# Casts and splits of q and k held behind the maximum and normalising of earlier steps

## The chip, the cores and the metric

The kernel runs on one core of one Trainium2 chip. The metric is the device time of one execution in microseconds; several runs are summed up by their median. The engines are named as in the profile: PE is TensorE, DVE is VectorE, ACT is ScalarE, POOL is GpSimd, and SP is SyncE, which here only issues transfers.

## What is computed

Windowed attention with a distance bias feeds a feed-forward layer with a convolution over the sequence. Sizes are 4 batches, 8 heads, 768 positions, head width 64, 8 global and 96 local keys, model width 512, inner width 1024; all in fp32.

```python
scores = scale * np.matmul(q, k.transpose(0, 1, 3, 2)) + bias     # bias: minus slope x distance
scores = np.where(is_global | is_local, scores, -1e9)
a = np.exp(scores - scores.max(-1, keepdims=True))
x = np.matmul(a / (a.sum(-1, keepdims=True) + 1e-9), v)           # heads side by side: (B, S, 512)
h = np.maximum(x @ w_in, 0.0)
conv_out = sum(conv_w[k] * hp[:, k:k + S] for k in range(3))       # hp: h padded by one row
out = (h / (1.0 + np.exp(-conv_out))) @ w_out
```

## The kernel before

**Tiling.** The attention is 32 jobs m: a batch, a half of its sequence (384 queries) and a pair of heads. A job has three steps of 128 queries, so there are 96 steps s. A step computes scores on TensorE (L372 ff.; L395 from job 9 on), the maximum of each head on VectorE (`maxima`, L404, operation at L412), exponentials on ScalarE (L426), the normalising by the reciprocal (L438) on POOL (L444), and up to step 31 half of it on ScalarE (L442). Two steps later its probabilities are transposed (L452) and evacuated (L457); when the three steps of a job are through, the product with v follows (L473, one PSUM buffer), of which a high part xh (ScalarE, L485) and a low part xl (VectorE, L489) are kept. The scores have two PSUM buffers, so a step's scores wait for the exponentials of the step two before.

**High and low parts.** A product in fp32 is made of three matmuls over rounded high parts and low rests. For the scores of jobs 9 to 31 (NATIVE is 9) `prep(m, part)` (L126) makes them: part 0 casts the keys into kk and the queries into qh on POOL (L137, L138), part 1 subtracts on VectorE, so that the lower half of kk holds the rest (L141), and makes ql (L142). `load(m)` (L93) fetches the raw keys rk and queries rq into one buffer each (L114, L115), `load_v(m)` (L118) fetches v into one of two (L123).

**Feed-forward.** When the four jobs of a half are done, its blocks go through the first product (L507, tile h), the rectifier (ScalarE, L517), three convolution taps (ScalarE L555 or POOL L557, then VectorE L558 and L559), tanh (L577), a check of range (L588), the gate (VectorE, L610), the split into gh (ScalarE, L612) and gl (VectorE, L613), the second product (L622) and its output (L629, L630). The weights are decoded in the first third of the run on VectorE (L316, L318, L320, L331) and POOL (L325); they are read again and compared near the end (L339 to L350).

**Order.** The program's main loop runs over the steps and calls the parts above. Steps below HAND (16) are issued in the order in which they are written. From step 16 on a scheduler orders each engine's queue from the dependences and its own timeline. `tc.issue_after(x)` adds one constraint: what is issued inside it and runs on the engine of x stands behind x in that engine's queue. `last_ttr[s]` is the last maximum of step s, on VectorE.

The loop calls `prep(m + 1)` in the first step of job m, and loads of job m + 2 in its second step (from m = 7 on):

```python
        if i == 0:
            prep(m + 1, 0)
            prep(m + 1, 1)
            if 1 <= m < NATIVE - 2:
                load(m + 2)
        elif i == 1 and m + 2 >= NATIVE:
            load(m + 2)
        if s >= NB and i == 0:
            load_v(m)
```

Of the kernel before, what the change touches and what calls it, by code (L numbers as in the profile page):

```python
# [15 lines left out]
ALU = mybir.AluOpType  # L16
# [9 lines left out]
NB = TB // P  # L26
# [12 lines left out]
HAND = 16  # L39
# [28 lines left out]
def fast_path(tc, io):  # L68
    nc = tc.nc
    V, A, G, T = nc.vector, nc.scalar, nc.gpsimd, nc.tensor  # L70
# [17 lines left out]
    p2 = pool("p2", 2)  # L88

    jobs = [(b, u, hp) for b in range(B) for u in range(2) for hp in range(NPAIR)]  # L90
    raw, qk, vt = {}, {}, {}

    def load(m):  # L93
        if m >= len(jobs):
# [23 lines left out]
    def load_v(m):  # L118
        if m >= len(jobs):
            return  # L120
        b, u, hp = jobs[m]
        t = p2.tile([P, NB, 2, P], F32, tag="v", name=f"v{m}")
        nc.sync.dma_start(t, io["vv"][b, u, hp].rearrange("p (i c d) -> p i c d", i=NB, c=2))  # L123
        vt[m] = t

    def prep(m, part):  # L126
        if m >= len(jobs) or m < NATIVE:
            return
        b, u, hp = jobs[m]
        w = NKC[u]  # L130
        rq, rk = raw[m]
        if part == 0:
            qh = p2.tile([P, 2 * TB], F32R, tag="qh", name=f"qh{m}")
            ql = p2.tile([P, 2 * TB], F32R, tag="ql", name=f"ql{m}")
            kk = p2.tile([P, 2 * w], F32R, tag="kk", name=f"kk{m}")
            qk[m] = (qh, ql, kk)
            G.tensor_copy(kk, rk)  # L137
            G.tensor_copy(qh, rq)  # L138
        else:
            qh, ql, kk = qk[m]  # L140
            V.tensor_tensor(kk[64:], rk[64:], kk[64:].bitcast(F32), ALU.subtract)  # L141
            V.tensor_tensor(ql, rq, qh.bitcast(F32), ALU.subtract)  # L142
# [226 lines left out]
    last_ttr = {}  # L369
# [64 lines left out]
    def normalise(s):  # L434
        pb, c0, n, mm = st_s[s]
        if s >= SHARED:
            V.tensor_scalar(mm[:, 4:6], mm[:, 2:4], 1.0e-9, None, ALU.add)
        V.reciprocal(mm[:, 6:8], mm[:, 4:6])  # L438
        for j in range(2):
            x, inv = pb[:, j, c0 : c0 + n], mm[:, 6 + j : 7 + j]  # L440
            if j and s < SHARED:
                A.activation(x, x, AF.Copy, scale=inv)  # L442
            else:
                G.tensor_scalar(x, x, inv, 1.0, ALU.mult, ALU.mult)  # L444

    def transposes(s):
        m, i = steps[s]
# [43 lines left out]
    def ends(s):  # L491
        return s >= 0 and s % NB == NB - 1
# [218 lines left out]
    def check_some(cost):  # L711
        pace[0] += cost
        while pace[1] < NCHK and pace[0] >= CHECK_EVERY * (pace[1] + 1):
            check_piece(pace[1])
            pace[1] += 1
    last_exp, last_mm, last_ev = {}, {}, {}

    def fill(k):
        with contextlib.ExitStack() as es:
# [65 lines left out]
    for s in range(len(steps) + LAG_V + 1):  # L785
        cur["s"] = s
        m, i = steps[s] if s < len(steps) else (len(jobs), -1)
        if s < HAND:
# [5 lines left out]
            x = (s - LAG_V - 1) // NB if ends(s - LAG_V - 1) else None  # L794
# [8 lines left out]
            if s:  # L803
                normalise(s - 1)
# [17 lines left out]
        else:  # L822
# [20 lines left out]
            if s <= len(steps):  # L843
                normalise(s - 1)
# [18 lines left out]
        if s == 0:  # L863
            for k in range(len(order)):
                chain(*order[k])
        elif s == 1:
            load_v(0)
            load(2)
# [1 line left out]
            if at == s:  # L870
                start_piece(k)
        if i == 0:
            prep(m + 1, 0)
            prep(m + 1, 1)
            if 1 <= m < NATIVE - 2:
                load(m + 2)
        elif i == 1 and m + 2 >= NATIVE:
            load(m + 2)
        if s >= NB and i == 0:
            load_v(m)  # L880
    fill(10**9)
# [133 lines left out]
def build(nc, io):  # L1015
    with tile.TileContext(nc, schedule_with_timeline_sim=True) as tc:
        fast_path(tc, io)
# [49 lines left out]
```

## Time and profile before

| what | value |
|---|---|
| median of 3 runs | 445.34 us (444.66 to 445.89) |
| the profiled execution, its own time | 445.31 us |
| its span, first to last instruction | 443.5 us |
| mean granted TensorE clock | 0.996 of full |
| TensorE busy | 431.2 us (97%) |
| VectorE busy | 357.2 us (81%) |
| ScalarE busy | 309.9 us (70%) |
| POOL busy | 221.2 us (50%) |

Busy times are of one engine; a transfer or another engine may run beside them. Times in the views count from the span's start. Matmuls are pipelined, so the durations of neighbours overlap and the distance of their starts is the shorter, more telling number. A bracket behind an instruction says how long its engine idled before it and which instruction ended that.

### The profile page before, as it was taken

What the parts mean: (1) busy time and instruction counts of PE and PEld (TensorE: products, weight loads), DVE (VectorE), ACT (ScalarE), POOL (GpSimd) and SP (SyncE); (2) the same over time, 40 slices, a digit from 0 to 9 for tenths busy, and PEclk for the clock granted to TensorE, in tenths of its full rate; (3) what the DMA queues carried; (4) which work ended last, traced back from release to release, by engine and by line L of the source; (5) the groups of instructions that cost most, each with busy time, mean ns of one, the idle gap of its engine ahead of it and who ended that gap; (6) DMA issues with size and microseconds to landing.
All of it is one profiled execution on the core that took longest, in us unless ns stands there. A gap on an engine that the chain in (4) does not pass through costs nothing.

```text
span 443.5 us, 9050 instructions
## 1 busy us (share of the span) xinstructions
PE 431.2 (97%) x3039; PEld 374.5 (84%) x3039; DVE 357.2 (81%) x935; ACT 309.9 (70%) x839; POOL 221.2 (50%) x307
## 2 busy tenths in 40 slices
PE   8988999799999999999999999999999999999996
PEld 7655778799889988899889988899988998798876
DVE  6899899998999988757998989747999975568700
ACT  4889988789896678546876865665776776755540
POOL 5555334654456786556757744647656841013000
PEclk9999999899999999999999999999999999999999
DMA  6998953141543244442246134423235313980111
GB/s 210 294 255 258 271 184 110 40 163 65 153 128 120 75 136 132 128 125 94 85 128 192 41 107 145 141 102 104 67 119 181 103 48 122 312 295 32 47 49 55
DMA packets 22662, 60.02 MB, mean 135 GB/s; under 512 B 3024, under 2 KB 5584, under 8 KB 22608
## 3 DMA queue, kind: packets, MB, share of 16 engines
q1 hardware_dynamic: 18992, 53.01, 39.2%
q10 hardware_dynamic: 3616, 6.36, 3.9%
q8 instruction: 26, 0.43, 0.4%
q14 instruction: 28, 0.23, 0.2%
HBM read 53.07 MB, written 6.29 MB: 134 GB/s over the span
## 4 chain that ended last, share of the span: by engine, by line
PE 81%; DVE 8%; DMA 6%; ACT 3%; issue 1%; POOL 0%; SPq 0%; DVEq 0%; ACTq 0%
PE o L622 26%; PE h L507 25%; PE pv L473 10%; PE t L452 9%; PE s L395 7%; DMA check<-in_w 3%; PE s L385 1%; PE last L643 1%; DMA out<-ob 1%; DVE w L320 1%; DVE w L318 1%; ACT junkb L350 1%; ACT pbuf L426 1%; DMA rq<-in_qk 1%; PE sb L385 1%
## 5 line engine op out<-in xcount | busy, mean ns | idle before, releaser
L444 POOL TENSOR_SCALAR pbuf<-pbuf,mm 128x232 f32<-128x232 f32 (+1 forms) x160 | 113.3, 718 | 81.0 <-DVE mm L438 49.5
L426 ACT ACTIVATE pbuf<-s,mm 128x232 f32<-128x232 f32 (+1 forms) x165 | 72.1, 442 | 48.3 <-DVE mm L412 34.6
L412 DVE CUSTOM_DVE_ANT_0 s<-s,tab 128x232 f32<-128x232 f32 (+1 forms) x165 | 63.1, 385 | 20.2 <-PE s L395 15.7
L622 PE MATMUL o<-woh,gh 128*128 128x512 f32 x184 | 74.1, 403 | 0.0
L622 PE MATMUL o<-woh,gl 128*128 128x512 f32 x184 | 73.5, 400 | 0.0
L622 PE MATMUL o<-wol,gh 128*128 128x512 f32 x184 | 73.3, 398 | 0.0
L452 PE MATMUL t<-ident,pbuf 128*128 128x128 f32 x384 | 65.4, 279 | 5.4 <-ACT pbuf L442 2.7
L557 POOL TENSOR_SCALAR c<-hbuf,cw 128x382 f32<-128x382 f32 (+1 forms) x48 | 38.6, 807 | 56.5 <-ACT hbuf L517 56.5
L452 PEld LDWEIGHTS t<-ident,pbuf 128*128 128x128 f32 x384 | 46.4, 141 | 20.2 <-ACT pbuf L442 6.4
L457 ACT ACTIVATE pt<-t 128x512 f32<-128x512 f32 x96 | 57.0, 597 | 8.3 <-PE t L452 8.0
L507 PE MATMUL h<-xl,wih 128*128 128x384 f32 x252 | 59.4, 343 | 0.0
L507 PE MATMUL h<-xh,wih 128*128 128x384 f32 x252 | 58.8, 347 | 0.1
L507 PE MATMUL h<-xh,wil 128*128 128x384 f32 x252 | 55.8, 339 | 0.0
L473 PE MATMUL pv<-pt,v 128*64 128x128 f32 (+1 forms) x768 | 50.3, 280 | 0.3 <-DVE xl L489 0.2
L473 PEld LDWEIGHTS pv<-pt,v 128*64 128x64 f32 (+1 forms) x768 | 42.5, 138 | 8.6 <-issue 3.6
L558 DVE SCALAR_TENSOR_TENSOR c<-hbuf,cw,c 128x382 f32<-128x382 f32 (+1 forms) x64 | 44.3, 699 | 4.8 <-POOL c L557 3.7
L559 DVE SCALAR_TENSOR_TENSOR c<-hbuf,cw,c 128x382 f32<-128x382 f32 (+1 forms) x64 | 45.4, 712 | 0.3
L507 PEld LDWEIGHTS h<-xh,wih 128*128 128x128 f32 x252 | 43.2, 190 | 2.1 <-ACT pbuf L426 0.9
L507 PEld LDWEIGHTS h<-xl,wih 128*128 128x128 f32 x252 | 43.9, 189 | 0.7 <-issue 0.7
L507 PEld LDWEIGHTS h<-xh,wil 128*128 128x128 f32 x252 | 44.1, 188 | 0.0
L517 ACT ACTIVATE hbuf<-h 128x384 f32<-128x384 f32 x64 | 31.4, 495 | 13.5 <-PE h L507 12.5
L622 PEld LDWEIGHTS o<-woh,gl 128*128 128x128 f32 x184 | 34.6, 188 | 7.3
(120 smaller groups left out, 856.1 us busy)
## 6 DMA issues: line engine op xcount, KB each, us to landing
v<-in_vv SPq DMA_DIRECT2D x32, 384.0 KB, 3.6
rq<-in_qk SPq DMA_DIRECT2D x23, 384.0 KB, 3.1
wr<-in_w SPq DMA_DIRECT2D x16, 512.0 KB, 5.3
check<-in_w SPq DMA_DIRECT2D x16, 512.0 KB, 4.9
rk<-in_qk SPq DMA_DIRECT2D x12, 504.0 KB, 3.6
out<-ob ACTq DMA_DIRECT2D x23, 256.0 KB, 2.4
rk<-in_qk SPq DMA_DIRECT2D x11, 408.0 KB, 3.6
rq<-in_qk SPq DMA_DIRECT2D x16, 96.0 KB, 5.1
```

The costliest lines, as they stand in the source:

```text
L412: last_ttr[s] = V.tensor_tensor_reduce(out=sp[j][:, c0 : c0 + n], in0=sp[j][:, c0 : c0 + n], in1=tb, scale=-0.125, scalar=3.0e38, op0=ALU. ...
L426: last_exp[s] = A.activation(pb[:, j, c0 : c0 + n], sp[j][:, c0 : c0 + n], AF.Exp, bias=mm[:, j : j + 1], scale=-1.0, accum_out=mm[:, 2 + ...
L444: G.tensor_scalar(x, x, inv, 1.0, ALU.mult, ALU.mult)
L452: T.transpose(pt[:, j, c, :], pb[:, j, c * P : (c + 1) * P], ident)
L457: last_ev[s] = A.activation(sb, st_pt[s], AF.Copy)
L473: T.matmul(pv[m][64 * j : 64 * j + 64, i * P : (i + 1) * P], vt[m][:n, i, c, 64 * j : 64 * j + 64], sb[:n, j, c, :], start=c == 0, stop=c ...
L507: T.matmul(ps[:, :TB], w_[:, k, fs], x_, start=part == 0 and k == 0, stop=part == 2 and k == NK - 1,)
L517: A.activation(half, ps[:, :TB], AF.Relu, scale=0.5)
L557: G.tensor_scalar(c, *tap(1), 1.0, ALU.mult, ALU.mult)
L558: V.scalar_tensor_tensor(c, *tap(0), c, ALU.mult, ALU.add)
L559: V.scalar_tensor_tensor(c, *tap(2), c, ALU.mult, ALU.add)
L622: last = T.matmul(ps, g_[:, f], w_[:, f], start=f == 0 and part == 0, stop=f == NF - 1 and part == 2,)
```

## The change

Two dictionaries are added, for the transfer of v of each job and the last normalising instruction on POOL of each step. From step 16 on, the casts and splits of job m + 1 are held behind the last maximum of the step before (on VectorE) and behind the normalising of the step two before (on POOL). The loads of q and k of job m + 2 are held behind the transfer of v of job m - 1 (on SP). `prep` does nothing below job 9, so it takes effect from step 24 on, and the loads from step 22 on. The instructions are the same.

```diff
     def load_v(m):
...
-        nc.sync.dma_start(t, io["vv"][b, u, hp].rearrange("p (i c d) -> p i c d", i=NB, c=2))
+        last_v[m] = nc.sync.dma_start(t, io["vv"][b, u, hp].rearrange("p (i c d) -> p i c d", i=NB, c=2))
...
     def normalise(s):
...
-                G.tensor_scalar(x, x, inv, 1.0, ALU.mult, ALU.mult)
+                last_scaled[s] = G.tensor_scalar(x, x, inv, 1.0, ALU.mult, ALU.mult)
...
         if i == 0:
-            prep(m + 1, 0)
-            prep(m + 1, 1)
+            with contextlib.ExitStack() as es:
+                if s >= HAND:
+                    es.enter_context(tc.issue_after(last_ttr[s - 1].ins))
+                    es.enter_context(tc.issue_after(last_scaled[s - 2].ins))
+                prep(m + 1, 0)
+                prep(m + 1, 1)
             if 1 <= m < NATIVE - 2:
                 load(m + 2)
         elif i == 1 and m + 2 >= NATIVE:
-            load(m + 2)
+            with tc.issue_after(last_v[m - 1].ins):
+                load(m + 2)
```

The scheduler answers with another order. In the rows below a name ends in the job or step it belongs to and a running number (kk10 is the key tile of job 10, s27 and mm27 the scores and maxima of step 27, w7 a weight being decoded). VectorE's queue around step 27, before:

```order
L412 ISA mm27_1290 128x1
L141 TENSOR_TENSOR kk10_1335<-rk10_1253,kk10_1335 64x816
L320 SCALAR_TENSOR_TENSOR w7_0_1250<-wr7_0_1010,w7_0_1250 128x512
L558 SCALAR_TENSOR_TENSOR c0_865<-hbuf_190,cw_185,c0_865 128x382
L412 ISA s27_1285,mm27_1290<-s27_1285,tab_166 128x136
L412 ISA mm27_1290 128x1
L438 RECIPROCAL mm26_1261<-mm26_1261 128x2
L316 TENSOR_SCALAR w7_1_1329<-wr7_1_1065 128x512
L331 TENSOR_TENSOR wol_189<-w6_1_1199,woh_188 128x512
L412 ISA s28_1342,mm28_1347<-s28_1342,tab_166 128x232
L412 ISA mm28_1347 128x1
L489 TENSOR_TENSOR xl6_1222<-pv6_1171,xh6_1221 128x384
```

And now, from the row in the same place on:

```order
L412 ISA s27_1285,mm27_1290<-s27_1285,tab_166 128x136
L412 ISA mm27_1290 128x1
L412 ISA s27_1285,mm27_1290<-s27_1285,tab_166 128x136
L412 ISA mm27_1290 128x1
L316 TENSOR_SCALAR w7_1_1329<-wr7_1_1065 128x512
L331 TENSOR_TENSOR wol_189<-w6_1_1199,woh_188 128x512
L318 SCALAR_TENSOR_TENSOR w7_1_1329<-wr7_1_1065,w7_1_1329 128x512
L412 ISA s28_1342,mm28_1347<-s28_1342,tab_166 128x232
L412 ISA mm28_1347 128x1
L558 SCALAR_TENSOR_TENSOR c0_865<-hbuf_190,cw_185,c0_865 128x382
L489 TENSOR_TENSOR xl6_1222<-pv6_1171,xh6_1221 128x384
L412 ISA s28_1342,mm28_1347<-s28_1342,tab_166 128x232
```

The two halves of step 27's maximum are neighbours now; the subtract for kk10 has left this place and follows behind xl6, as does L559; the decode L318 has moved ahead of xl6, and L320 of w7_0 ahead of step 27.

TensorE's queue at step 29, before (h1 and o are tiles of the two products, pv7 the values of job 7, t24 to t26 the transposes of steps):

```order
L507 MATMUL h1_2_1439<-xh6_1221,wih_186 128x384
L452 MATMUL t24_1270<-ident_153,pbuf0_193 128x128 x4
L395 MATMUL s29_1399<-kk9_1204,qh9_1202 128x232
L395 MATMUL s29_1399<-kk9_1204,ql9_1203 128x232
L395 MATMUL s29_1399<-kk9_1204,qh9_1202 128x232
L395 MATMUL s29_1399<-kk9_1204,ql9_1203 128x232
L473 MATMUL pv7_1299<-pt23_1233,v7_1068 64x128 x4
L473 MATMUL pv7_1299<-pt21_1133,v7_1068 64x128 x4
L473 MATMUL pv7_1299<-pt22_1192,v7_1068 64x128 x4
L452 MATMUL t25_1315<-ident_153,pbuf1_194 128x128 x4
L507 MATMUL h1_1_1413<-xh4_945,wih_186 128x384
```

And now:

```order
L507 MATMUL h1_2_1439<-xh5_1080,wih_186 128x384
L452 MATMUL t25_1315<-ident_153,pbuf1_194 128x128 x4
L507 MATMUL h1_0_1370<-xh4_945,wih_186 128x384
L507 MATMUL h1_0_1370<-xh5_1080,wih_186 128x384
L507 MATMUL h1_0_1370<-xh6_1221,wih_186 128x384
L507 MATMUL h1_2_1439<-xh6_1221,wih_186 128x384
L395 MATMUL s29_1399<-kk9_1204,qh9_1202 128x232
L395 MATMUL s29_1399<-kk9_1204,ql9_1203 128x232
L395 MATMUL s29_1399<-kk9_1204,qh9_1202 128x232
L395 MATMUL s29_1399<-kk9_1204,ql9_1203 128x232
L473 MATMUL pv7_1299<-pt23_1233,v7_1068 64x128 x4
L473 MATMUL pv7_1299<-pt21_1133,v7_1068 64x128 x4
```

The transposes of step 25 stood behind the values of job 7 and now stand ahead of step 29's scores, which the values follow.

VectorE's queue around steps 39 to 41, before (gl0_3 and gl0_4 are low parts for the second product, c1 a tile of the convolution):

```order
L142 TENSOR_TENSOR ql14_1955<-rq14_1866,qh14_1954 128x768
L610 SCALAR_TENSOR_TENSOR hbuf_190<-c1_1541,hbuf_190 128x8x2
L610 SCALAR_TENSOR_TENSOR hbuf_190<-c1_1541,hbuf_190 128x8x128 x2
L437 TENSOR_SCALAR mm38_1874<-mm38_1874 128x2
L412 ISA s39_1903,mm39_1908<-s39_1903,tab_166 128x232
L412 ISA mm39_1908 128x1
L489 TENSOR_TENSOR xl11_1974<-pv11_1917,xh11_1973 128x384
L613 TENSOR_TENSOR gl0_2_1577<-hbuf_190,gh0_2_1576 128x8x2
L438 RECIPROCAL mm38_1874<-mm38_1874 128x2
L141 TENSOR_TENSOR kk14_1956<-rk14_1865,kk14_1956 64x1008
L412 ISA s39_1903,mm39_1908<-s39_1903,tab_166 128x232
L412 ISA mm39_1908 128x1
```

And now:

```order
L613 TENSOR_TENSOR gl0_2_1577<-hbuf_190,gh0_2_1576 128x8x2
L613 TENSOR_TENSOR gl0_3_1851<-hbuf_190,gh0_3_1850 128x1024
L438 RECIPROCAL mm38_1874<-mm38_1874 128x2
L613 TENSOR_TENSOR gl0_4_1947<-hbuf_190,gh0_4_1946 128x1024
L141 TENSOR_TENSOR kk14_1956<-rk14_1865,kk14_1956 64x1008
L412 ISA s40_1963,mm40_1968<-s40_1963,tab_166 128x232
L412 ISA mm40_1968 128x1
L437 TENSOR_SCALAR mm39_1908<-mm39_1908 128x2
L412 ISA s41_2018,mm41_2023<-s41_2018,tab_166 128x232
L412 ISA mm41_2023 128x1
L489 TENSOR_TENSOR xl11_1974<-pv11_1917,xh11_1973 128x384
L142 TENSOR_TENSOR ql14_1955<-rq14_1866,qh14_1954 128x768
```

The low half xl11 stood behind the first half of step 39's maximum; now both halves of step 39, a third L610, two L613, the subtract for kk14 and the first halves of steps 40 and 41 are ahead of it. The split ql14 was ahead of it and has gone behind.

## Rows read from the trace of the kernel before

**Rows 1.** The page: busy time of the engines, and two rows of its 40 slices.

```profile
PE 431.2 (97%) x3039; PEld 374.5 (84%) x3039; DVE 357.2 (81%) x935; ACT 309.9 (70%) x839; POOL 221.2 (50%) x307
...
PE   8988999799999999999999999999999999999996
...
DVE  6899899998999988757998989747999975568700
```

**Rows 2.** Busy time in windows of 20 us; columns as in its header.

```profile
core 0: us, PE busy (x) PEld busy (x) DVE busy (x) ACT busy (x) POOL busy (x), PEclk, DMA share, GB/s
...
80.00:100.00 20.00, 17.70 (x133) 16.62 (x133) 19.85 (x44) 15.57 (x43) 10.48 (x10) 0.91 0.35 114
...
120.00:140.00 20.00, 20.00 (x138) 17.51 (x138) 19.61 (x43) 16.45 (x39) 11.30 (x12) 1.00 0.42 134
```

**Rows 3.** Waits of TensorE: engine line, what it waited for, us, times, longest.

```profile
PE s L395 <- ACT pbuf L426: 2.1, 1, 2.1
```

**Rows 4.** Busy time in two short windows, columns as in rows 2.

```profile
85.10:88.40 3.30, 3.30 (x28) 2.97 (x29) 3.30 (x8) 1.84 (x5) 0.75 (x1) 0.54 0.00 0
38.00:39.60 1.60, 0.56 (x5) 0.32 (x4) 1.60 (x5) 1.36 (x6) 0.00 (x0) 1.00 1.00 237
```

**Rows 5.** Timeline, 80 to 90 us: start, us, engine, line; in brackets what it waited for.

```profile
80.27 1.24 DVE L141 TENSOR_TENSOR kk<-rk,kk 64x816 fp32r<-64x816 f32 x1
...
81.49 0.60 PE L452 MATMUL t<-ident,pbuf 128*128 128x128 f32 x4
...
82.30 0.60 DVE L558 SCALAR_TENSOR_TENSOR c<-hbuf,cw,c 128x382 f32<-128x382 f32 x1
...
82.83 0.29 DVE L412 CUSTOM_DVE_ANT_0 s<-s,tab 128x136 f32<-128x136 f32 x1
...
84.15 0.38 PE L395 MATMUL s<-kk,qh 128*128 128x232 f32 x1 [2.06 <-ACT pbuf L426]
...
85.10 2.61 PE L473 MATMUL pv<-pt,v 128*64 128x128 f32 x24 [0.24 <-DVE xl L489]
...
86.18 0.68 DVE L318 SCALAR_TENSOR_TENSOR w<-wr,w 128x512 int32<-128x512 int32 x1
...
87.75 0.49 ACT L485 ACTIVATE xh<-pv 128x384 fp32r<-128x384 f32 x1 [1.30 <-PE pv L473]
...
89.54 0.42 PE L507 MATMUL h<-xh,wih 128*128 128x384 f32 x1
```

**Rows 6.** Timeline, 76 to 82 us, POOL.

```profile
76.10 1.15 POOL L137 CAST kk<-rk 128x816 fp32r<-128x816 f32 x1 [0.50 <-DMA rk<-in_qk]
...
80.62 1.21 POOL L444 TENSOR_SCALAR pbuf<-pbuf,mm 128x232 f32<-128x232 f32 x1
```

**Rows 7.** Timeline, 128 to 138 us, VectorE, then TensorE.

```profile
128.69 1.10 DVE L142 TENSOR_TENSOR ql<-rq,qh 128x768 fp32r<-128x768 f32 x1
...
132.26 0.35 DVE L437 TENSOR_SCALAR mm<-mm 128x2 f32<-128x2 f32 x1
...
132.83 0.55 DVE L489 TENSOR_TENSOR xl<-pv,xh 128x384 fp32r<-128x384 f32 x1
...
133.57 1.21 DVE L141 TENSOR_TENSOR kk<-rk,kk 64x1008 fp32r<-64x1008 f32 x1
...
137.66 0.39 DVE L412 CUSTOM_DVE_ANT_0 s<-s,tab 128x232 f32<-128x232 f32 x1
...
137.98 1.62 DVE L613 TENSOR_TENSOR gl<-hbuf,gh 128x1024 fp32r<-128x1024 f32 x1
...
134.00 0.42 PE L507 MATMUL h<-xl,wih 128*128 128x384 f32 x1
134.26 0.86 PE L507 MATMUL h<-xh,wil 128*128 128x384 f32 x4
```

**Rows 8.** Waits of VectorE from 60 to 120 us, the longest.

```profile
DVE s L412 <- PE s L395: 1.3, 1, 1.3
```

**Rows 9.** Timeline, 85 us: a tap on VectorE and a cast on POOL.

```profile
84.96 1.30 DVE L559 SCALAR_TENSOR_TENSOR c<-hbuf,cw,c 128x382 f32<-128x382 f32 x1
84.98 0.86 POOL L137 CAST kk<-rk 128x816 fp32r<-128x816 f32 x1 [0.49 <-PE s L395]
```

More of the change, by code (lines that the diff above doesn't have):

```diff
@@ L90, in fast_path @@
     jobs = [(b, u, hp) for b in range(B) for u in range(2) for hp in range(NPAIR)]
-    raw, qk, vt = {}, {}, {}
+    raw, qk, vt, last_v = {}, {}, {}, {}
     def load(m):
@@ L715, in check_some @@
             pace[1] += 1
-    last_exp, last_mm, last_ev = {}, {}, {}
+    last_exp, last_mm, last_ev, last_scaled = {}, {}, {}, {}
     def fill(k):
```

## Prediction

> **What bounds the kernel now.** I read the page first: TensorE is busy 97% of the span, VectorE 81% [rows 1]. So the time is TensorE's work plus whatever TensorE waits. The page's row of slices (11 us each) shows TensorE full from the fifth slice on but for the eighth and the last, and VectorE nearly full up to the fifteenth, with gaps after it [rows 1]. The change first acts at step 24, in the seventh slice. The windows of 20 us then give the size: from 80 to 100, 17.70 of 20.00 us are busy and the granted clock falls to 0.91; from 120 to 140 TensorE is full [rows 2]. The same rows show the second thing that matters: VectorE is busy 19.85 and 19.61 of 20.00 there, so its queue has nothing to give. The list of TensorE's waits names the hole: one wait of 2.1 us of scores (L395) for the exponentials (L426) [rows 3]. A short window behind it shows what followed: 3.30 us at a mean clock of 0.54, so nearly all of it at the 1.2 GHz level instead of 2.4 [rows 4]. That is 3.30 x 0.46 = 1.52 us lost, beside 2.06 + 0.24 = 2.30 us idle [rows 5]. All that can be won there is **3.8 us**; nothing else of this size is left on TensorE behind step 24.
>
> Why the hole is there, is read from the timeline around it [rows 5]. Step 29's scores start at 84.15, when the exponentials of step 27 have freed the score buffer. Those came late since the second maximum of step 27 ran only at 82.83: ahead of it on VectorE stood the subtract for job 10's keys (L141, 80.27, 1.24 us) and a convolution tap (L558, 82.30, 0.60 us). Neither was needed by then.
>
> **The change, part by part.** No instruction is added or removed; the waits it adds are on order alone. The executed time is 445.31 us, the span 443.5 with 1.8 us around it; the median of the runs is 445.34, so the sum holds for both. A difference of 0.3% (1.34 us) is about what a measurement of this kernel can tell from none.
>
> *The hole at 82.* In the new order the two halves of step 27's maximum stand side by side, and the subtract of job 10 comes after the low half xl6. The second half thus ends 1.24 + 0.60 = 1.84 us earlier, at about 81.3, and step 29's scores need not wait for VectorE any more. What is late next is xl6, for which the values (L473) wait: its queue loses the subtract (1.24) and gets one weight decode (L318, 0.68) in its place [rows 5]. So the values, which started at 85.10 on its end, can start at 85.10 - 0.56 = 84.5. By then four transposes of step 25 that came after the values are done, too: the four at 81.49 took 0.60 with the last one's tail, so 0.44 or so of TensorE's time [rows 5]. At full clock the values and three matmuls take about 2.0 us, to 86.5. Then TensorE waits for xh7 (L485), which stands on ScalarE behind step 28's last exponentials, a tap and an evacuation. Those can start when VectorE has done the maximum behind xl6, 0.5 us after it, at 85.05; four operations of xh7's own length or a little more (0.49 [rows 5], I take 0.55) end at 87.25, and the next matmul starts at about 87.4. Before, that matmul ran at 89.54 [rows 5] with 0.44 us of transposes done that now come later. Gain: 89.54 - 87.4 - 0.44 = **1.7 us**. If the clock falls again, the values and three matmuls take 2 us longer, and the gain is about 1.0. The bounds are 0 and 3.8.
>
> *Loads (SP).* Key and query loads now follow a load of v in SP's queue, which waits for its buffer. The cast that needs the data is later, too: job 10's ran at 76.10, as soon as its load had come, and now stands behind step 25's normalising, which ended at 80.62 + 1.21 = 81.83 [rows 6]. That is 5.7 us in which the load may come later at no cost. Without that cover POOL's queue would stand still for the load, as it did for 0.50 us before that cast; once or twice that is the upper end, and nothing the value that I take.
>
> *Casts (POOL).* They move behind the normalising of the step two before. POOL's normalising before them comes earlier, that behind them later: the transposes of step 26 must wait for two casts more. TensorE's order has them 19 matmuls of the first product later, which at 0.17 us each (four take 0.86, the tail of the last 0.34 among it [rows 7]) is 3.3 us of cover for two casts of 1.15 us [rows 6]. Cost nothing; at most 2 us if that cover were gone.
>
> *The splits of q (VectorE) at step 39 to 41.* Here lies the cost. Before, xl11 ran at 132.83 and TensorE used it at 134.00 [rows 7]. Now it stands behind all that ran from 133.57 to 137.98 + 1.62 = 139.60 (the subtract for job 14, two halves of maxima, L610, two L613): 6.03 us without a gap. To this come 0.19 us up to 133.57, one more half of a maximum (0.39) and an addition (0.35, as at 132.26); the split ql14 (1.10) has left. So xl11 starts at 132.83 + 6.03 + 0.19 + 0.39 + 0.35 - 1.10 = 138.7 and ends 0.55 later at **139.2**. TensorE has more ahead of it as well: seven matmuls of h at 0.17, four of scores, and ten transposes at 0.11, together 1.2 + 0.5 + 1.1 + 0.2 for changes between kinds = 3.0 us, so it would arrive at 137.0. That is a wait of **2.2 us**, in one piece or spread over the waits ahead of it (scores of step 41 for exponentials of step 39, xh11 behind them on ScalarE).
>
> *How the two meet.* If TensorE gains 1.7 us at 88, it only arrives earlier at 139, and waits as much longer, unless VectorE gains too. VectorE's queue can gain only what it idles: from 88 to 128 one wait of 1.3 us for scores [rows 8]. So what counts at 139 is VectorE: 2.2 late less 1.3 regained is **+0.9 us** on the old schedule; TensorE's earlier gain does not survive it. A short wait of step 36's scores behind the moved split ql12 (between 0 and that split's time, some 1.1; I take 0.4) only shifts where TensorE waits, since VectorE sets the end at 139. Behind the fifteenth slice VectorE has gaps [rows 1] into which a later split can slip, so I cost the later jobs at nothing; without such gaps each could cost what this one does, up to 0.9. The weight check at the end is started by TensorE's progress, so it shifts along.
>
> Sum: 445.3 + 0.9 = **446.2 us**, on the upper side of no change.
>
> **A rule on the shared port.** VectorE's durations carry the argument at 139, and they vary: a tap took 0.60 us at 82.30 [rows 5], and one of the same shape 1.30 us at 84.96 with a cast on POOL beside it [rows 9]. The Trainium skill (GPSIMD Engine Reference, section 1. Specifications) says that POOL shares its SBUF interfaces with VectorE and contends with VectorE instructions that read two SBUF inputs; the taps, the subtracts, L610 and L613 are such. Those two rows agree. The casts are as many as before, but now run in pairs; if that adds two such meetings to VectorE's full queue before 139, it is 2 x 0.70 = 1.4 us more: a rival below.
>
> **Rivals.**
> 1. *Hidden at 139.* VectorE's operations meet fewer casts, or the split comes up sooner than my row-by-row sum, and the gain at 82 is kept: between 445.3 - 1.7 = 443.6 and 445.3 - 3.8 = 441.5, most likely 443.4. For it: each term at 139 is an order of instructions, timed with rows of the old order. Against: VectorE is busy 98% there.
> 2. *Slower (the other side).* The wait at 133 to 139 is long enough that the clock falls there too, as it did after 82: 2.2 us more of wait plus 1.5 of lower clock less 1.3 regained, 445.3 + 2.4 = 447.7. It decides from a hole of about the size of the old one; but at 38.0 to 39.6 TensorE was busy for 0.56 of 1.60 us and the clock stayed at 1.00 [rows 4], so a shorter hole need not do it.
> 3. *More meetings of VectorE and POOL*: two taps more before 139 at 1.30 instead of 0.60 us [rows 5, 9], 446.2 + 1.4 = 447.6.
> 4. *Nothing moves.* The waits trade places one for one, or the gain is small and shows nowhere: 445.3.
>
> **How the numbers follow.** The forecast (446.2, give or take 1.2) has 0.36; rival 1 has 0.29, rival 2 0.16, rival 3 0.08, rival 4 0.11. Of the forecast's 0.36 I count 0.25 within 0.3% (444.0 to 446.7), 0.10 slower and 0.01 faster; of rival 1 0.26 faster and 0.03 within; of rivals 2 and 3 0.22 slower and 0.02 within; rival 4 within. That is faster 0.27, same 0.41, slower 0.32. The range reaches through the likelier half of rival 1 and through rivals 2 and 3: 442.7 to 448.2; left out are the full recovery below it and a fall of the clock with both losses above it. The forecast's own range is 445.0 to 447.4.
>
> **What would show it.** In the changed profile: the one wait of scores L395 for exponentials of 2.1 us should be gone or under 0.7, the window 80 to 100 should show TensorE above 17.7 and the clock above 0.91; the values after step 29 should wait for xl (L489) instead, and the next h for xh (L485), under 1.2 us each. In 120 to 140 TensorE should be busy some 18 of 20 us, not all of it, with waits on ScalarE or xl; VectorE's 1.3 us wait near 104 should be gone. I am wrong if TensorE stays full from 130 to 140 (then rival 1), if the clock falls there (rival 2), or if the hole at 82 is still there (rival 4).

## The result and the profile after

The changed kernel takes **451.7 us** (median of 4 runs, 451.4 to 452.8) against 445.3 us: a ratio of 1.0148, 95% interval 1.0126 to 1.017. It is slower by 1.5%, outside the range of the prediction (442.7 to 448.2).

Executions of one kernel differ in the granted clock of TensorE, and the time goes with it. Beside the experiments below the kernel before ran 85 times: it took 444.1 us (median) in the 18 runs with a mean clock of 0.999 or 1.00, 445.4 in the 34 with 0.995 or 0.996, and 447.0 in the 29 with 0.991 or 0.992. The change took 451.5 us in its three runs with 0.999 or 1.00, so at equal clock it costs 7.4 us.

The page of the changed kernel, the lines that answer to [rows 1] (PE is TensorE, DVE is VectorE, ACT is ScalarE):

```profile
span 450.6 us, 9071 instructions
...
PE 433.2 (96%) x3039; PEld 373.8 (83%) x3039; DVE 363.7 (81%) x935; ACT 307.8 (68%) x839; POOL 224.4 (50%) x307
...
PE   8888999799898999999999999999999999999997
```

The work is the same, the span 7.1 us longer. TensorE is full again from the fourteenth slice on, so the loss lies ahead of some 150 us. Its windows there, which answer to [rows 2] (columns as there):

```profile
80.00:100.00 20.00, 18.14 (x135) 16.58 (x137) 19.74 (x40) 16.02 (x43) 11.41 (x10) 1.00 0.28 82
100.00:120.00 20.00, 18.22 (x140) 16.40 (x136) 18.42 (x46) 15.91 (x46) 6.90 (x9) 1.00 0.35 112
120.00:140.00 20.00, 18.48 (x133) 15.20 (x134) 18.87 (x44) 18.67 (x49) 11.54 (x12) 1.00 0.38 118
140.00:160.00 20.00, 18.76 (x132) 17.67 (x131) 16.30 (x42) 9.10 (x28) 14.75 (x20) 1.00 0.38 120
```

And of the kernel before, the two of these windows that were not shown:

```profile
100.00:120.00 20.00, 20.00 (x156) 18.22 (x155) 18.18 (x48) 18.45 (x51) 8.57 (x13) 1.00 0.36 102
...
140.00:160.00 20.00, 20.00 (x156) 18.70 (x153) 19.40 (x50) 14.50 (x42) 16.32 (x20) 1.00 0.24 68
```

From 80 to 100 us the change wins, as it was meant to: 0.44 us more busy, and no low clock. From 100 to 160 TensorE then idles 1.78 + 1.52 + 1.24 = 4.54 us, where before it was full. VectorE is busy about as long as before from 100 to 140 (37.29 against 37.79 us), but less behind it: 16.30 instead of 19.40 us. So it isn't that VectorE was kept from working up to 140 us. I read it this way: it did other work first, TensorE came late, and then VectorE had to wait. The longest row of its waits from 60 to 160 us in the change, and the same row of the kernel before:

```profile
DVE mm L437 <- ACT pbuf L426: 4.0, 6, 1.1
```

```profile
DVE mm L437 <- ACT pbuf L426: 0.4, 1, 0.4
```

An addition that needs a step's exponentials held its queue for 4.0 us instead of 0.4, 3.0 us of it behind 140 us.

TensorE's waits from 60 to 160 us (engine line <- what ended the wait: us in total, times, longest). Before there was one wait for exponentials of 2.1 us [rows 3] and one for xl of 0.2. Now:

```profile
PE s L395 <- ACT pbuf L426: 2.9, 4, 1.8
PE t L452 <- POOL pbuf L444: 1.8, 3, 0.9
PE pv L473 <- DVE xl L489: 0.8, 1, 0.8
PE h L507 <- ACT xh L485: 0.7, 2, 0.6
PE h L507 <- ACT hbuf L517: 0.5, 1, 0.5
```

That is 6.7 us in 11 waits instead of 2.3 us in two. Behind 160 us follow 0.7 us in two waits, which were none before: 4.4 + 0.7 = 5.1 us more by the list. A stall costs more than the list says, since a listed wait begins only when the tail of the matmul ahead of it has ended: the four transposes ahead of the old wait of 2.06 us have 0.60 us in their row, but use 0.44 or so of TensorE's time [rows 5]. By the starts of the matmuls in the traces I get 2.3 us more than listed for the 13 stalls of the change, and 0.3 us for the two before. 5.1 + 2.0 = 7.1 us is what the two spans differ by; the low clock in these two executions does not change that, as it cost 1.5 us behind the old hole in the one and 1.6 us near 40 us in the other (last section). So the loss is in these stalls. The medians are only 6.4 us apart, as most runs of the kernel before have some low clock and three of the change's four next to none.

### The profile page after: what moved, and what is told of

Its sections match the earlier page's. It is cut to its first block, busy times and chain, and to the rows that moved or that the text cites. A ratio compares the mean times of both kernels' runs of the same rounds, so it can differ in the third digit from the quotient of the medians.

```text
span 450.6 us, 9071 instructions
## 1 busy us (share of the span) xinstructions
PE 433.2 (96%) x3039; PEld 373.8 (83%) x3039; DVE 363.7 (81%) x935; ACT 307.8 (68%) x839; POOL 224.4 (50%) x307
## 4 chain that ended last, share of the span: by engine, by line
PE 74%; DVE 15%; ACT 7%; issue 2%; POOL 1%; DMA 1%; ACTq 0%; POOLq 0%; DVEq 0%
PE h L507 25%; PE o L622 23%; PE pv L473 8%; PE t L452 7%; PE s L395 5%; ACT pbuf L426 3%; DVE s L412 3%; PE s L385 2%; DVE hbuf L610 2%; DVE c L558 2%; DVE kk L141 2%; PE last L643 1%; PE sb L385 1%; ACT pt L457 1%; DVE gl L613 1%
## 5 line engine op out<-in xcount | busy, mean ns | idle before, releaser
L444 POOL TENSOR_SCALAR pbuf<-pbuf,mm 128x232 f32<-128x232 f32 (+1 forms) x160 | 118.3, 749 | 118.1 <-DVE mm L438 68.9
L452 PE MATMUL t<-ident,pbuf 128*128 128x128 f32 x384 | 63.7, 280 | 7.3 <-ACT pbuf L442 3.7
L452 PEld LDWEIGHTS t<-ident,pbuf 128*128 128x128 f32 x384 | 44.6, 140 | 22.9 <-ACT pbuf L442 6.4
L557 POOL TENSOR_SCALAR c<-hbuf,cw 128x382 f32<-128x382 f32 (+1 forms) x48 | 35.3, 736 | 51.5 <-ACT hbuf L517 46.7
L507 PE MATMUL h<-xh,wih 128*128 128x384 f32 x252 | 58.6, 344 | 1.2 <-ACT xh L485 0.7
L507 PE MATMUL h<-xl,wih 128*128 128x384 f32 x252 | 58.4, 341 | 0.1
L507 PE MATMUL h<-xh,wil 128*128 128x384 f32 x252 | 56.9, 342 | 0.0
L507 PEld LDWEIGHTS h<-xh,wih 128*128 128x128 f32 x252 | 43.1, 189 | 4.0 <-ACT xh L485 1.2
L507 PEld LDWEIGHTS h<-xl,wih 128*128 128x128 f32 x252 | 43.9, 188 | 0.7 <-issue 0.3
L507 PEld LDWEIGHTS h<-xh,wil 128*128 128x128 f32 x252 | 44.1, 188 | 0.0
L559 DVE SCALAR_TENSOR_TENSOR c<-hbuf,cw,c 128x382 f32<-128x382 f32 (+1 forms) x64 | 43.0, 676 | 0.6
L622 PEld LDWEIGHTS o<-woh,gh 128*128 128x128 f32 x184 | 34.7, 189 | 6.9 <-issue 0.7
```

Source lines behind the costliest of these rows:

```text
L444: last_scaled[s] = G.tensor_scalar(x, x, inv, 1.0, ALU.mult, ALU.mult)
L452: T.transpose(pt[:, j, c, :], pb[:, j, c * P : (c + 1) * P], ident)
L507: T.matmul(ps[:, :TB], w_[:, k, fs], x_, start=part == 0 and k == 0, stop=part == 2 and k == NK - 1,)
L557: G.tensor_scalar(c, *tap(1), 1.0, ALU.mult, ALU.mult)
L559: V.scalar_tensor_tensor(c, *tap(2), c, ALU.mult, ALU.add)
L622: last = T.matmul(ps, g_[:, f], w_[:, f], start=f == 0 and part == 0, stop=f == NF - 1 and part == 2,)
```

## The experiments

Each ratio is against runs of the kernel before in the same session, whose medians were 445.2 to 447.0 us; so the ratios compare better than the times.

**The three parts of the change apart.** First the hold on POOL alone:

```diff
             with contextlib.ExitStack() as es:
                 if s >= HAND:
-                    es.enter_context(tc.issue_after(last_ttr[s - 1].ins))
                     es.enter_context(tc.issue_after(last_scaled[s - 2].ins))
...
-            with tc.issue_after(last_v[m - 1].ins):
-                load(m + 2)
+            load(m + 2)
```

> Only the hold on POOL (casts behind the normalising of two steps before); no hold on VectorE, none on the loads. The theory that this hold alone carries the loss expects the time of the whole change, 451.5 us (450.5 to 452.5). The rival that the hold on VectorE or the loads' hold costs a part expects less, 446 to 450.

Measured: 452.7 us, ratio 1.0137 (1.0082 to 1.0192). The queues of TensorE, VectorE, ScalarE and POOL stand in exactly the order of the whole change. Then the rest of the change without it (the maxima's hold and the loads):

> Only the holds on VectorE and on the loads. The order of every engine but SP is that of the kernel before, and on SP one transfer (q of job 9) stands elsewhere. The theory that the POOL hold alone carries the loss expects 445.3 us (444.6 to 446.0). The rival that the hold costs by itself (an added wait in the queue, a load that comes late) expects 447 or more.

Measured: 445.5 us, ratio 0.998 (0.9954 to 1.0005). So the POOL hold carries the whole loss. The hold on the maxima moves nothing in any queue, the loads' hold one transfer on SP, and neither costs. Third, the POOL hold with `s >= 45` instead of `s >= HAND`:

> The POOL hold only from step 45 on (job 16 on), none before. The theory that the loss is made where VectorE's queue is full (up to about 160 us, before step 45) expects 445.3 us, at most 446.3, with no TensorE wait over 0.6 us added behind 160 us. The rival that the hold costs wherever it acts, in proportion to the jobs (16 of 23), expects 449 to 450.

Measured: 446.0 us, ratio 0.9998 (0.9969 to 1.0027). Of the 23 jobs with casts, the holds for the last 16, behind some 160 us, where VectorE has gaps, cost nothing that this interval can tell.

The profile of the POOL hold alone has the clock at 1.00 throughout, so it is the clean trace of the changed order. Its timeline around the old hole, to set beside [rows 5]:

```profile
78.25 0.97 PE L507 MATMUL h<-xh,wih 128*128 128x384 f32 x4 [0.52 <-ACT hbuf L517]
...
79.93 0.68 DVE L331 TENSOR_TENSOR wol<-w,woh 128x512 fp32r<-128x512 f32 x1
...
81.69 0.81 POOL L325 CAST woh<-w 128x512 fp32r<-128x512 f32 x1
81.95 1.09 DVE L331 TENSOR_TENSOR wol<-w,woh 128x512 fp32r<-128x512 f32 x1
82.45 1.28 POOL L138 CAST qh<-rq 128x768 fp32r<-128x768 f32 x1
82.97 1.31 DVE L318 SCALAR_TENSOR_TENSOR w<-wr,w 128x512 int32<-128x512 int32 x1
84.08 0.38 PE L395 MATMUL s<-kk,qh 128*128 128x232 f32 x1 [0.33 <-ACT pbuf L426]
...
85.05 0.54 DVE L489 TENSOR_TENSOR xl<-pv,xh 128x384 fp32r<-128x384 f32 x1
...
85.64 1.54 PE L473 MATMUL pv<-pt,v 128*64 128x128 f32 x24 [0.85 <-DVE xl L489]
...
88.48 0.44 PE L507 MATMUL h<-xh,wih 128*128 128x384 f32 x1 [0.58 <-ACT xh L485]
```

The 2.06 us wait is 0.33, and three others stand around it (0.52, 0.85, 0.58): 2.28 us together, where 2.30 stood before. What is won here is mostly the low clock. And where step 36's scores wait:

```profile
116.23 0.39 DVE L412 CUSTOM_DVE_ANT_0 s<-s,tab 128x232 f32<-128x232 f32 x1
116.55 0.95 DVE L142 TENSOR_TENSOR ql<-rq,qh 128x768 fp32r<-128x768 f32 x1
117.42 0.39 DVE L412 CUSTOM_DVE_ANT_0 s<-s,tab 128x232 f32<-128x232 f32 x1
...
118.41 0.45 ACT L426 ACTIVATE pbuf<-s,mm 128x232 f32<-128x232 f32 x1
118.98 0.17 DVE L437 TENSOR_SCALAR mm<-mm 128x2 f32<-128x2 f32 x1 [0.75 <-ACT pbuf L426]
119.00 0.37 PE L395 MATMUL s<-kk,qh 128*128 128x232 f32 x1 [1.76 <-ACT pbuf L426]
```

The moved split ql12 stands between a maximum half of step 35 and the second half of step 34, so step 34's last exponentials begin at 118.41 and TensorE has waited 1.76 us. The split takes 0.87 us of VectorE's time there (116.55 to 117.42), about half of that wait; what else made it was not traced. Behind it VectorE waits too (0.75 us, for the same exponentials), then TensorE again, at 129.88 (0.48 us), and here:

```profile
136.21 1.93 DVE L613 TENSOR_TENSOR gl<-hbuf,gh 128x16 fp32r<-128x16 f32 x2
...
136.90 0.37 PE L395 MATMUL s<-kk,qh 128*128 128x232 f32 x1 [0.21 <-ACT pbuf L426]
137.77 0.45 PE L507 MATMUL h<-xh,wih 128*128 128x384 f32 x1 [0.16 <-ACT xh L485]
138.07 0.15 DVE L438 RECIPROCAL mm<-mm 128x2 f32<-128x2 f32 x1
...
138.41 2.63 POOL L444 TENSOR_SCALAR pbuf<-pbuf,mm 128x232 f32<-128x232 f32 x2 [1.34 <-DVE mm L438]
139.72 0.44 PE L452 MATMUL t<-ident,pbuf 128*128 128x128 f32 x2 [0.29 <-POOL pbuf L444]
141.10 0.44 PE L452 MATMUL t<-ident,pbuf 128*128 128x128 f32 x2 [0.94 <-POOL pbuf L444]
141.57 0.55 DVE L489 TENSOR_TENSOR xl<-pv,xh 128x384 fp32r<-128x384 f32 x1
```

The transposes wait for POOL, POOL for VectorE's reciprocal, and ahead of the reciprocal stands feed-forward work (two L613, 1.93 us). The normalising is slow, too: its two instructions take 2.63 us while VectorE runs L613 and L141, where two of the same form take 0.89 us at 144.71 beside maxima. That suggests that a meeting of POOL and VectorE is part of the 0.94 us. The late xl11 at 141.57 is waited for by nobody.

**Which jobs.** The POOL hold for a few jobs only, jobs 9 and 10, 11 and 12 (steps 30, 33) and 13 to 15 (steps 36, 39, 42):

```diff
-                if s >= HAND:
+                if s in (24, 27):
                     es.enter_context(tc.issue_after(last_scaled[s - 2].ins))
```

> The POOL hold for the casts of jobs 9 and 10 alone (steps 24 and 27). The theory that each stretch pays by its own waits expects the hole at 82 us without the low clock, but with short waits for rectifier, exponentials, xl and xh (some 2.9 us in all as in the changed kernel), nothing added behind 100 us: 444.0 to 446.0 us. The rival that the loss behind 100 us is a late effect of this first stretch (VectorE pushed back for good) expects waits at step 36 and steps 39 to 41 here too, and 448 or more.

> The POOL hold for jobs 11 and 12 alone (steps 30 and 33). The first theory expects the old hole at 82 us as it was, and new waits at about 101 (transposes for POOL, 0.8) and at step 36's scores (1.9): 447.0 to 448.5 us. The rival of the late effect expects neither: 445.3.

> The POOL hold for jobs 13 to 15 alone (steps 36, 39 and 42). The first theory expects the old hole, and the waits at steps 39 to 41 alone (0.7 + 2.2 us): 447.5 to 449 us. The rival of the late effect expects 445.3.

Measured: 450.3 us, ratio 1.0109 (1.0068 to 1.015); 448.7, 1.0087 (1.0056 to 1.0117); 448.8, 1.0067 (1.0034 to 1.01). The parts add up to more than the whole, and the waits need not be where the held jobs are. With jobs 11 and 12 the first new one is at 127 us, some 20 us behind the last held cast (106.22); with jobs 9 and 10 the longest lie behind 117 us, where nothing is held:

```profile
119.30 0.37 PE L395 MATMUL s<-kk,qh 128*128 128x232 f32 x1 [0.95 <-ACT pbuf L426]
122.99 0.37 PE L395 MATMUL s<-kk,qh 128*128 128x232 f32 x1 [0.88 <-ACT pbuf L426]
128.44 0.44 PE L452 MATMUL t<-ident,pbuf 128*128 128x128 f32 x2 [1.76 <-POOL pbuf L444]
```

The scheduler answers one moved piece with another order behind it, on every engine, and here it is that order that costs, not the hold in its place. (With jobs 13 to 15 the new waits, at 130 and 145 us, are among the held steps.)

**Which cast.** The hold around the query cast (L138) alone, as here, and around the key cast (L137) alone, with nothing else of the change:

```diff
-            G.tensor_copy(kk, rk)
-            G.tensor_copy(qh, rq)
+            held = (lambda: tc.issue_after(last_scaled[cur["s"] - 2].ins)) if cur["s"] >= HAND else contextlib.nullcontext
+            with contextlib.nullcontext():
+                G.tensor_copy(kk, rk)
+            with held():
+                G.tensor_copy(qh, rq)
```

> The POOL hold on the query casts alone, for all jobs; the key casts are free. The theory that the late splits of q on VectorE (ql12 between the halves of steps 35 and 34, ql14 and its neighbours at step 39 to 41) carry most of the loss expects 449 us or more. The rival that the key part, the first of the two casts and subtracts, carries it expects under 447.

> Only the key cast of each job is held behind the normalising on POOL, not the query cast (the query cast alone under the hold gave 445.5, as the kernel before). If the two parts act separately, the key casts carry the whole loss: 451 to 453. If it takes both, or if the size is a matter of which order the scheduler happens to choose: between 446 and 450. The order has xl11 4.2 us of work later and xl12 4.6 later.

Measured: 445.5 us, ratio 1.0017 (0.9993 to 1.0042), and 447.9 us, 1.0064 (1.0033 to 1.0094). By the ratios some two fifths of the loss come with the key casts and little or none with the query casts (at a clock of 0.999 or 1.00 they took 3.6 and 1.1 us more than the kernel before); the rest comes only with both. My idea that the late query splits carry it fell.

**Splits late, casts free.** No hold on POOL. The two subtracts of each job are issued one step later, behind that step's last maximum (first diff); or, milder, behind the last maximum of the same step (second diff); or so for step 27 alone.

```diff
-            prep(m + 1, 1)
+            if s < 24:
+                prep(m + 1, 1)
...
+        if i == 1 and s >= 24:
+            with tc.issue_after(last_ttr[s].ins):
+                prep(m + 1, 1)
```

```diff
-            prep(m + 1, 1)
+            with tc.issue_after(last_ttr[s].ins) if s >= 24 else contextlib.nullcontext():
+                prep(m + 1, 1)
```

> No hold on POOL; the casts stay where they were in the program, but the two subtracts of the next job are written one step later and held behind that step's last maximum on VectorE. The theory that late splits on a full VectorE queue make the loss expects 448 us or more, with TensorE waiting between 100 and 145 us. The rival that the casts ahead of later normalising on POOL make it (transposes that wait for POOL) expects 444 to 446, with no transposes waiting for POOL.

> The kernel before, with all subtracts of the next job held behind the last maximum of the step that writes them, casts and loads free. The hole at 82 should go as with job 10 alone; ahead of the second halves of steps 33 to 38 stands no more than before, only xl11 has 4 us more ahead. If xl11 is the one loss left, about 1.5 to 2.5 us gained and 1 to 2 us lost: 443.5 to 446. The rival that any new order of the full queue costs 3 us or more expects 448 or more.

> The kernel before, with the subtracts of job 10 alone held behind step 27's own last maximum (the hold of the change names the step before and binds nothing there). The key subtract so leaves the place ahead of step 27's second half. If that place makes the hole at 82 us, the 2.1 us wait shrinks under 1.0 and the clock stays up: a gain of 1.5 to 2.5 us at 90 us. The scheduler then also puts xl11 behind some 3 us of other work and step 36's second half behind 2.7; if VectorE's full queue makes each of these a wait, they take 1 to 3 us back: 443.5 to 447. The rival of a clean gain expects 441.5 to 443.

Measured: 453.2 us, 1.0123 (1.0068 to 1.0177); 446.6 us, 1.0019 (0.9987 to 1.0051); 446.2 us, 1.0009 (0.9981 to 1.0038). Late splits can cost a large part of this without any cast held: three of the four runs had a mean clock of 0.989 or less, and the one with 0.996 took 450.6 us against 445.4 of the kernel before. The two mild forms left the hole at 82 as it was and won nothing. A fourth kernel adds to the milder form that feed-forward work stands behind the latest xl (`last_xl[0]` is set where xl is made):

```diff
+                if last_xl and HAND <= cur["s"] <= len(steps):
+                    es.enter_context(tc.issue_after(last_xl[0].ins))
```

> As the run before, and the feed-forward work held behind the latest low part xl on VectorE. It takes taps and gates from ahead of the maxima of steps 27 to 36 (1 to 3 us less ahead of each), but xl11 still has 4.4 us more ahead. If urgent work ahead of the rest is what counts, this is the fastest of the four, 442 to 445; if it only starves the gate and the second product, 447 or more.

Measured: 452.5 us, 1.0148 (1.0092 to 1.0203). It moved the loss into one wait of the values for xl, 3.9 us.

**One late low half in the old order.** The kernel before, with xl11 alone held behind the last maximum of step 40; run twice:

```diff
-        V.tensor_tensor(xl, pv[m], xh.bitcast(F32), ALU.subtract)
+        with tc.issue_after(last_ttr[40].ins) if m == 11 else contextlib.nullcontext():
+            V.tensor_tensor(xl, pv[m], xh.bitcast(F32), ALU.subtract)
```

> The kernel before, with one low part (xl11) held behind step 40's last maximum, so that it stands about where the changed kernel has it; up to there every queue is as before. If VectorE's order around steps 39 to 41 is what costs, xl11 ends near 140 us instead of 133.4, TensorE has 3 us of other work to put ahead and waits 2.5 to 3 us: 447.5 to 448.5 us. The rival that TensorE's own new order hides it expects 445.3.

> The kernel before with the one low half xl11 held behind the last maximum of step 40, as before. Its time was 452.4 while its profile showed only 3.7 us of waits for it and for what is behind it. If the rest was low clock by chance: 449 to 450 here. If it belongs to the order: 452 again, and a profile at clock 0.99 or above shows waits of over 6 us behind 130 us.

Measured: 452.4 us both times, 1.0146 (1.0091 to 1.0202) and 1.0159 (1.0112 to 1.0206). Two rows of the second profile, and the two windows behind (one line was added, so L508 is L507 and L490 is L489):

```profile
135.61 0.63 PE L452 MATMUL t<-ident,pbuf 128*128 128x128 f32 x4 [1.48 <-ACT pt L457]
140.34 0.44 PE L508 MATMUL h<-xl,wih 128*128 128x384 f32 x1 [2.41 <-DVE xl L490]
```

```profile
139.00:142.00 3.00, 1.66 (x7) 1.66 (x8) 3.00 (x9) 1.28 (x5) 1.64 (x2) 0.86 0.00 0
142.00:145.00 3.00, 3.00 (x15) 2.64 (x16) 2.79 (x8) 1.85 (x7) 3.00 (x4) 0.58 0.26 57
```

3.9 us of waits, and 3.00 x 0.42 = 1.3 us of low clock behind them. The profiled execution (450.2 us, mean clock 0.996) was the fastest of the four; the others (452.1 to 453.2) had 0.989, and 0.007 of a span of 450 us is 3 us, so what they are longer by is low clock. The run shows what one instruction on VectorE that TensorE needs can cost in this stretch; it does not show that xl11 is what costs under the change.

**Repairs of the changed kernel.** First the split that step 36 waits for: job 12's subtracts one step later, behind the last maximum of step 34.

```diff
                 prep(m + 1, 0)
-                prep(m + 1, 1)
+                if s != 33: prep(m + 1, 1)
...
+            if s == 34:
+                with tc.issue_after(last_ttr[34].ins):
+                    prep(m + 1, 1)
```

> The whole change, with the two splits of job 12 on VectorE issued one step later and behind the last maximum of step 34, so that the split ql12 no longer stands ahead of it; step 36's scores then should not wait 1.8 us near 120. Theory A (the single waits of TensorE add up, since TensorE's work is fixed): 451.7 - 1.5 = about 450.2, if no other wait takes its place. Theory B (VectorE's whole queue sets the pace, as my prediction had it, and a wait of scores only shifts): 451.7 as the change, with a wait of the same size behind 120. The order behind job 12 moves as well (the low half xl12 stands 3.8 us of work later), so anything from 449.5 to 453 can come; the place of the waits tells more than the time.

Measured: 452.5 us, 1.0143 (1.0094 to 1.0192): nothing won. The wait of 1.76 us is gone, and these stand in its place:

```profile
118.06 0.37 PE L395 MATMUL s<-kk,ql 128*128 128x232 f32 x1 [0.68 <-DVE ql L142]
...
135.37 0.44 PE L452 MATMUL t<-ident,pbuf 128*128 128x128 f32 x2 [0.81 <-POOL pbuf L444]
141.08 0.35 PE L395 MATMUL s<-kk,qh 128*128 128x232 f32 x1 [1.26 <-DVE kk L141]
```

No single wait is the loss. The result is also what theory B expected, a wait that only shifts; since the order behind job 12 moved as well, this run does not part the two theories. Second, the feed-forward work of a step held behind the reciprocal of the step before on VectorE, from step 16 on (`last_rcp[s]` is the reciprocal of step s, p the step before):

```diff
+                if p in last_rcp and cur['s'] >= HAND:
+                    es.enter_context(tc.issue_after(last_rcp[p].ins))
                 for last in (last_ttr, last_exp, last_mm):
```

> The whole change, and from step 16 on the feed-forward work of a step is held behind the reciprocal of the step before on VectorE. By the order the second halves of the maxima of steps 30 to 35 and 40 stand 1 to 5 us of work earlier than under the change alone, while xl11 stays late (4.6 us of work later than in the kernel before). Theory A (the loss is urgent maxima and reciprocals behind feed-forward work): 447 to 449, waits for the exponentials and the normalising between 115 and 142 under 1 us in all. Theory C (the loss is the late low half xl11, or POOL's late casts, which both stay): 451 to 453.

Measured: 450.8 us, 1.011 (1.0062 to 1.0158). The window 100 to 120 is full again, and the one behind it pays:

```profile
100.00:120.00 20.00, 20.00 (x155) 18.14 (x153) 18.53 (x51) 17.47 (x47) 9.39 (x11) 1.00 0.40 124
120.00:140.00 20.00, 16.63 (x112) 13.50 (x109) 19.48 (x47) 16.79 (x46) 13.72 (x15) 1.00 0.40 124
```

The time lies between the two theories. Urgent work behind feed-forward work is thus shown as a part of it at most: about 1 us of 6 by the medians, and the intervals of the two overlap.

**The gain without the new order.** The POOL hold for job 10 alone (`if s == 27:`), which frees step 27's second maximum from the keys' subtract and leaves the queues behind step 31 nearly as before.

> The hold behind the normalising on POOL for the casts of job 10 alone (step 27), nothing else of the change. By the order the second maximum of step 27 loses the subtract for job 10's keys ahead of it as under the change, but behind step 31 VectorE's queue is nearly that of the kernel before (differences up to 1.5 us of work, against 5 under the change; xl11 stands where it stood). If the loss of the change is the new order in the full stretch from 100 to 145 us and the gain at 82 is real: 442.5 to 444.5, the 2.06 us wait of step 29's scores under 1 us and TensorE full from 100 to 160. If the gain at 82 is taken back by the waits that took its place under the change (xl6, xh7): 445 to 446. If any new order in this stretch costs: above 447.

Measured: 446.3 us, 1.0014 (0.9995 to 1.0032). Its three longest waits of TensorE from 60 to 160 us:

```profile
PE t L452 <- POOL pbuf L444: 1.0, 1, 1.0
PE pv L473 <- ACT pt L457: 0.9, 1, 0.9
PE s L395 <- ACT pbuf L426: 0.8, 1, 0.8
```

The hole of 2.1 us shrank to 0.8, and the clock stayed up. But new waits, 1.9 us of them at 115.83 and 137.38, took the gain back, and not the waits for xl6 and xh7 that I had named for that case (445 to 446 us). At a clock of 0.999 or 1.00 it took 446.0 us against 444.1, so at equal clock it is slower by nearly 2 us, and the better clock of its runs hides that.

**All kernels side by side.** The waits of TensorE in the list from 60 to 160 us, all its rows added, beside the median and the median of the runs with that clock (- where none had it):

| kernel | waits, us | median, us | at clock 0.999 or 1.00 (runs) |
|---|---|---|---|
| before | 2.3 | 445.3 | 444.1 (18) |
| POOL hold from step 45 | 2.3 | 446.0 | 445.0 (1) |
| maxima's hold and loads | 2.6 | 445.5 | - |
| query casts | 3.2 | 445.5 | 445.3 (6) |
| splits behind own maximum | 3.6 | 446.6 | 446.4 (3) |
| job 10 | 3.8 | 446.3 | 446.0 (7) |
| keys of job 10 behind maximum 27 | 4.2 | 446.2 | 445.7 (3) |
| jobs 11 and 12 | 5.0 | 448.7 | 448.5 (1) |
| jobs 13 to 15 | 5.1 | 448.8 | 448.6 (1) |
| key casts | 5.3 | 447.9 | 447.8 (8) |
| change, feed-forward behind reciprocal | 5.8 | 450.8 | 450.8 (4) |
| xl11 late (two profiles) | 6.1, 6.9 | 452.4 | - |
| change, job 12's splits late | 6.2 | 452.5 | 452.0 (2) |
| feed-forward behind xl | 6.3 | 452.5 | - |
| splits late | 6.5 | 453.2 | - |
| POOL hold alone | 6.6 | 452.7 | 451.8 (2) |
| the change | 6.7 | 451.7 | 451.5 (3) |
| jobs 9 and 10 | 7.4 | 450.3 | 450.3 (4) |

Every kernel that moved work in this stretch waits more than the kernel before, and by and large the time goes with the waits, whatever was moved; each wait is of one profiled execution, and each costs up to 0.25 us more than its row, so many short ones cost more than few long ones. None is shown to be faster than before.

## Why the prediction was wrong, step by step

- **The hole at 82: right in kind, mis-sized.** Its marks came: the scores' wait fell from 2.06 to 0.33 us, the clock was 1.00, TensorE was busy for 18.1 us, xl and xh became the next waits (0.85 and 0.58). But the values started at 85.64, not at 84.5. The 1.1 us are two decodes on VectorE: L331 took 1.09 and L318 1.31 us while POOL cast a weight and the query; I had taken 0.68 for L318 [rows 5]. L331 takes 0.68 us at 79.93, where no cast runs, so the two are 0.41 + 0.63 = 1.04 us longer. That is rival 3's mechanism, at another place than I gave it: the rule that POOL contends with VectorE instructions that read two SBUF inputs (the Trainium skill, GPSIMD Engine Reference, section 1. Specifications) agrees with these rows. Not every meeting costs VectorE, though: the tap of 0.60 us that I took as undisturbed ran beside a cast too (L325, from 82.44), but had started before it. By my own sum the gain of 1.7 us is 89.54 - 88.48 - 0.44 = 0.6 us.
- **Loads, and the hold on the maxima: right.** Alone they cost nothing.
- **Casts on POOL "cost nothing": wrong in effect.** Transposes waited 1.8 us for the normalising. At 138 the normalising itself waited 1.34 us for the reciprocal on VectorE, so there it is VectorE's order that came late, and the normalising then ran at a third of its pace beside L613 and L141.
- **The waits at 133 to 139: close in size and place, wrong in the releaser.** I forecast 2.2 us for xl11 or spread over scores and xh11; the rows from 136.90 to 141.10 add up to 1.6 us. But most of it is the normalising of step 38, and xl11, though at 141.57 later than my 138.7, held nobody up.
- **"How the two meet": the step that failed.** I let one sum decide, how late VectorE is at 139, and held that a wait of step 36's scores (0.4 us) "only shifts where TensorE waits". It was 1.76 us and came on top: by 143 TensorE had waited at eleven places. The half of that step that held is that a gain at 82 does not survive; job 10's run shows that, for other waits than I had in mind. The half that fell is that VectorE's total sets the price: it gave +0.9 us, and the stalls grew by 7.1. VectorE was busy about as long up to 140 us, and from 60 to 140 it ran as many taps (28), gates (7), L613 (6) and decodes (21) in the profile of the POOL hold alone as before. But it ran 36 halves of maxima instead of 38, 6 low halves xl instead of 7 and 5 splits ql instead of 6: a split or feed-forward work stood where a maximum or a reciprocal was due, TensorE came late, and from 140 to 160 VectorE in turn was busy for 3.1 us less than before. What TensorE had lost by then no later stretch gave back. (VectorE idled 2.2 us from 88 to 128 before, not the 1.3 of its longest wait alone, so the sum was also short of what VectorE could regain.) That this order is the cause is read from the rows; of the two repairs one won nothing and the other about 1 us.
- **Later jobs at nothing: right** within the measurement when held alone; in the whole change they show 0.7 us of waits.
- **Rival 2**, the clock, did not decide: from 100 to 160 us it was 1.00. In the kernel with xl11 late it did fall behind the 2.41 us wait, so it can happen in this stretch.

Left open: how the scheduler's own timeline led it to these orders, and which of the moved instructions cost how much.

## What to carry to other kernels

A constraint given to a scheduler is not a local edit: count what its new order does to every queue that is full, well behind the place you meant. Where a second engine is as full as VectorE here (19.85 and 19.61 of 20.00 us), the sum of its work tells little; go through the places at which the first engine waits for it, and ask at each what the new order puts ahead of the one instruction that is due. And win a stall only where the engine behind it has slack to keep the gain.

## What was not expected of the hardware

The same hole does not always bring the clock down. From 38.0 to 39.6 us both kernels run the same instructions, with TensorE busy for 0.56 of 1.60 us [rows 4]. Behind it the granted clock stayed at 1.00 in the profiled execution before (first row), and was at the lower level, 1.2 GHz, at first in that of the change:

```profile
40.00:42.00 2.00, 2.00 (x29) 1.54 (x28) 1.97 (x6) 1.70 (x7) 1.98 (x2) 1.00 0.80 165
...
38.00:39.60 1.60, 0.56 (x4) 0.31 (x4) 1.60 (x5) 1.37 (x6) 0.00 (x0) 1.00 1.08 233
40.00:42.00 2.00, 2.00 (x16) 1.43 (x18) 1.97 (x6) 1.68 (x7) 1.99 (x2) 0.50 0.63 157
42.00:44.00 2.00, 2.00 (x19) 1.53 (x15) 1.20 (x5) 1.01 (x4) 1.55 (x2) 0.71 0.71 225
```

That is 1.0 + 0.6 = 1.6 us, about what the profiled execution of the change (452.8) is longer than its other three (451.4 to 451.9), whose mean clock was 0.999 or 1.000 against 0.995. The other way round, the kernel with xl11 late has the old 2.1 us wait at 82 and, in one of its two profiles, no low clock behind it:

```profile
80.00:100.00 20.00, 17.22 (x142) 16.23 (x141) 19.85 (x43) 15.75 (x43) 9.09 (x10) 1.00 0.35 110
```

So the 1.5 us of low clock that I counted into the hole were not always there to be won: in 18 of 85 runs the kernel before had a mean clock of 0.999 or 1.00.
